# Four transformer layers on one core: VectorE's order in the full layers written out by urgency, and the weight check queued later

## The chip, the cores and the metric

The kernel runs on one core of one Trainium2 chip. The metric is the device time of one execution in microseconds (us); lower is better. Five engines work side by side, each takes its own instructions in their order: TensorE (PE, with its weight loads as PEld), VectorE (DVE), ScalarE (ACT), GpSimd (POOL) and SyncE (SP), which issues nearly all DMA transfers here. An instruction waits on semaphores until what it reads is there and what it overwrites is free.

## The reference

Four attention layers follow each other on x of shape [2048, 512]. Layers 0 and 2 use the weights A and see a window of 256 keys, layers 1 and 3 use the weights B and see all 2048 keys. There are 32 heads of 16.

```python
x = x + A(layernorm(x));  x = x + B(layernorm(x))
x = x + A(layernorm(x));  x = x + B(layernorm(x))

def A(x):  # B is the same without the mask
    q, k, v = (x @ wqkv) split into 32 heads of 16
    scores = q @ k.T / 4
    scores = where(0 <= i - j < 256, scores, -1e9)
    return (softmax(scores) @ v, heads joined) @ wo
```

## The kernel before, in words

**Numbers.** Weights and normalized inputs are split into a high and a low float16 part, and a product is the sum of three of the four part products (TERMS, L369). The kernel also checks its assumptions on the data: the smallest and largest softmax sum and the largest weights by column. All of it ends in one flag, and if the flag is not set, a slower general path computes the result.

**The full layers (1 and 3).** The loops run over four chunks of 512 queries (c) and eight groups of four heads (qd); in layer 3 the head groups are taken two at a time. For each of 16 key tiles there are two exps: 8 score matmuls into a PSUM tile of two banks (`exps`, L655 to L673, matmul line L664), one ScalarE exp over 128x1024 (L672), and 16 matmuls of values times exps that accumulate in two PSUM banks, `acc` (L716). After 16 key tiles `epilogue` (L624) adds the two halves of acc (`sa`, a join: two VectorE operations, L373 and L374), transposes them (L635), divides by the softmax sum (L638 to L645), transposes back (L648) and splits the result into float16 parts (L650, L651).

**Side work.** What the next layer needs is put between the exps: the output projection `wo` (L589) with residual add (L600) and the statistics of the next norm (L384, L385), `norm` (L387: scales by a Newton iteration, L45 to L51, then for each of four tiles two normalized copies and a difference, L398 and L404), the DMA transposes of the result (L425), and the projections of queries and keys (`project`, L433) and of values (`values`). In a full layer all side products share one PSUM tile, `halves` (L338, handed out by `bank`, L340). A product's first matmul may only start when the last product has been read out by the join on VectorE. `project` then splits j into two float16 parts (L465, L466), squares them (POOL, L471) and writes them to DRAM; `squares` (L484) and its readers get maxima of key and query norms, and the key maxima (km, L509) are taken from it.

**The weight check.** `verify` (L303) takes the eight matrices in turn. For each it loads four column blocks of 256 KB, one after another, into one buffer (`wc`, DMA at L309, `bufs=1`), and reduces each with one VectorE operation (L311); then it transposes the result (L314), reduces it again (L316) and updates the running minimum and maximum (L317, L318). That is 32 loads and 32 reduces. The check's works (CW) stand in the list of layer 1's side works, `side1`, and the first one depends on ("Q", 1, 2), the queries of chunk 2, which are made at the start of layer 1. The check's result is read only by the flag at the end.

**What sets the order.** The program is recorded by a planner with an estimated clock (`clock[0]`). In a full layer, each two exps move it to at least 1.8 us after the last two (L953). A side work is a generator that yields after each matmul or asks for a pause (`wait`); `Side.step` and `share` (L869 to L900) take from the list of works what is ready and what the budget for this step allows. PE executes in the order in which the planner recorded it (`manual_schedule`, L206). The other engines, VectorE among them, are ordered by the framework's own scheduler, which works from priorities (`high_priority(HEAD_START)` lifts urgent joins) and from its own estimate of the durations. So a VectorE instruction may be put ahead of ones that were recorded before it. All orders are fixed when the program is built.

`epilogue` is recorded through the queue `pvq`; `flush` empties it. `T` transposes a normalized chunk from the time XNR on, which `norm` sets to the planner's clock + 9 us.

Of the kernel before, what the change touches and what calls it, by code (L numbers as in the profile page):

```python
# [189 lines left out]
def fast_path(ctx, tc, flag, a_x, a_wqkv, a_wo, b_wqkv, b_wo, out):  # L190
# [29 lines left out]
    def wait(us):  # L220

        return "wait", clock[0] + us


# [78 lines left out]
    def verify(ty, s):  # L303

        am = vp.tile([P, D], F32, name=f"wa{ty}_{s}", tag="wa", bufs=1)
        for k in range(NC):
            f = slice(k * P, (k + 1) * P)
            raw = vp.tile([P, NC, P], F32, name=f"wc{ty}_{s}_{k}", tag="wc", bufs=1)
            nc.sync.dma_start(raw, mats[ty, s][:, f].rearrange("(k p) f -> p k f", p=P))  # L309
            yield wait(16)  # L310
            nc.vector.tensor_reduce(am[:, f], raw.rearrange("p k f -> p f k"), axis=AX.X, op=ALU.max, apply_absolute_value=True)  # L311
            yield wait(3)
        at = vp.tile([P, D], F32, name=f"wt{ty}_{s}", tag="wc", bufs=1)
        nc.vector.transpose(at, am)  # L314
        mx = vp.tile([P, D // 32], F32, name=f"wx{ty}_{s}", tag="wx")
        nc.vector.tensor_reduce(mx, at.rearrange("p (b r) -> p b r", r=32), axis=AX.X, op=ALU.max)  # L316
        nc.vector.tensor_tensor(wlow, wlow, mx, ALU.min)  # L317
        nc.vector.tensor_tensor(whigh, whigh, mx, ALU.max)  # L318
        yield wait(3)

# [50 lines left out]
    def join(dst, ps, scale=1 / WS):  # L371

        nc.vector.tensor_scalar(dst, ps[0], scale, None, op0=ALU.mult)  # L373
        nc.vector.scalar_tensor_tensor(dst, ps[1], scale, dst, op0=ALU.mult, op1=ALU.add)  # L374
# [12 lines left out]
    def norm(l, c, xs, tail=False):  # L387

        mv = ST[l, c][1]
        y = rsqrt(nc, vp, f"{l}_{c}", mv[:, :, 1])  # L390
        if tail:
            nb = vp.tile([P, 4], F32, name=f"nb{l}_{c}", tag="lnb", bufs=1)
            nc.vector.scalar_tensor_tensor(nb, mv[:, :, 0], -1.0, y, op0=ALU.mult, op1=ALU.mult)
        out = []
        for i in range(4):
            xn = vp.tile([P, D], F32, name=f"xn{l}_{c}_{i}", tag="xn", bufs=1)
            xh = vp.tile([P, 2, D], F16, name=f"xh{l}_{c}_{i}", tag="xh", bufs=XNB)
            norm1 = lambda o: nc.vector.tensor_scalar(o, xs[i], mv[:, i, 0:1], y[:, i:i + 1], op0=ALU.subtract, op1=ALU.mult)  # L398
            norm1(xn)
            if tail:  # L400
                nc.scalar.activation(xh[:, 0], xs[i], AF.Identity, bias=nb[:, i:i + 1], scale=y[:, i:i + 1])
            else:
                norm1(xh[:, 0])
            nc.vector.tensor_tensor(xh[:, 1], xn, xh[:, 0], ALU.subtract)  # L404
# [5 lines left out]
        return out  # L410

# [21 lines left out]
    def project(l, s, c, act, ht=None):  # L433
# [13 lines left out]
        for t in range(NHT) if ht is None else (ht,):  # L447
            ps = bank()
            w0 = t * P if ht is None else 0
            yield from mms(ps, [(w[:, k, a, w0:w0 + P], xc[:, b, k, :]) for a, b in TERMS for k in range(NC)], 2.2)  # L450
            if not PH["full"]:
                settle(not sqs)
            sp = vp.tile([P, 2, QC], F16, name=f"sp{n}_{t}", tag="sp", bufs=3)
            with tc.high_priority(HEAD_START):
                if PH["full"]:
                    j = vp.tile([P, QC], F32, name=f"j{n}_{t}", tag="j")
                    join(j, (ps[:, 0], ps[:, 1]))
                else:
                    if act:
# [4 lines left out]
            if PH["full"]:  # L464
                nc.vector.tensor_copy(sp[:, 0], j)  # L465
                nc.vector.tensor_tensor(sp[:, 1], j, sp[:, 0], ALU.subtract)  # L466
            sq = vp.tile([P, QC], BF16, name=f"sq{n}_{t}", tag="sq", bufs=NHT)
            if act:
                nc.scalar.activation(sq, sp[:, 0], AF.Square)
            else:  # L470
                nc.gpsimd.tensor_tensor(sq, sp[:, 0], sp[:, 0], ALU.mult)  # L471
            sqs[t] = sq

            d = dst[8 * t:8 * t + 8].rearrange("h (d b) n -> (h d) b n", b=4)
            if s:
                nc.sync.dma_start(d[:, 0:2], sp[:, 0:1].broadcast_to([P, 2, QC]))
                nc.sync.dma_start(d[:, 2], sp[:, 1])
            else:
                nc.sync.dma_start(d[:, 0:2], sp)
                nc.sync.dma_start(d[:, 2], sp[:, 0])  # L480
            yield -MM if PH["full"] else -12 * MM
        return sqs

    def squares(n, sqs):  # L484

        ph = bank()
        for t, sq in sqs.items():
# [101 lines left out]
    def wo(l, c, tail):  # L589
# [4 lines left out]
        for i in range(4):  # L594
# [6 lines left out]
            nc.sync.dma_start(xd[k], xs[i])  # L601
            stats(l + 1, c, i, xs[i])
            if i == 3:
                XN[l + 1, c] = norm(l + 1, c, xs, tail)
            yield -MM if PH["full"] else -12 * MM

    def wo_part(c, t):
# [6 lines left out]
        for i in range(4):  # L614
            ps = bank()
            yield from mms(ps, [(o[:, a, i * P:(i + 1) * P], w[:, b, :]) for a, b in TERMS])
            k = 4 * c + i
            with tc.high_priority(HEAD_START):
                for p in ((ps[:, 0], ps[:, 1]) if PH["full"] else (ps,)):
                    nc.vector.scalar_tensor_tensor(xs[i], p, 1 / WS, xs[i], op0=ALU.mult, op1=ALU.add)  # L620
            nc.sync.dma_start(out[0, k * P:(k + 1) * P, :] if t == NHT - 1 else xd[k], xs[i])
            yield -MM

    def epilogue(l, c, qd, a):  # L624
# [3 lines left out]
        n = f"{l}_{c}_{qd}"  # L628
        t, u = divmod(qd, 2)
        ot = vp.tile([P, QC // 32, 32], F32, name=f"ot{n}", tag="oe")  # L630
        with tc.high_priority(HEAD_START if l % 2 else 0):
            if l % 2:
                a = vp.tile([P, QC], F32, name=f"sa{n}", tag="j")
                join(a, acc, 1.0)
            nc.vector.transpose(ot.rearrange("p b r -> p (b r)"), a)  # L635
        den = ot[:, :, DH]

        nc.vector.tensor_tensor(lmin, lmin, den, ALU.min)  # L638
        nc.vector.tensor_add(lsum, lsum, den)
        r = vp.tile([P, QC // 32], F32, name=f"r{n}", tag="r")  # L640
        nc.vector.tensor_scalar_max(r, den, L_MIN)
        nc.vector.reciprocal(r, r)
        if u == 0:
            OT[t] = vp.tile([P, QC // 32, 2, DH], F32, name=f"op{n}", tag="op", bufs=1)
        nc.vector.tensor_tensor(OT[t][:, :, u, :], ot[:, :, :DH], r[:, :, None].broadcast_to([P, QC // 32, DH]), ALU.mult)  # L645
        if u:
            o = vp.tile([P, QC], F32, name=f"o{n}", tag="o", bufs=1)
# [4 lines left out]
            ONR[l, c, t] = clock[0] + 4.5  # L652


# [165 lines left out]
    class Side:  # L820
# [13 lines left out]
        def one(self, force=False):  # L834

            if PH["full"] and PH["busy"]:
                return self.piece(PH["last"])
# [84 lines left out]
    def attention(l, works):  # L922
# [5 lines left out]
        for t in range(NHT if l == 3 else 1):  # L928
            for c in range(NQ):
# [10 lines left out]
                for qd in qds:  # L940
# [5 lines left out]
                    began, u = clock[0], 0  # L946
                    for f in (attn_win if win else attn_full)(l, c, qd, *ops, a):
                        if f is None:
                            flush(1)
# [12 lines left out]
                        elif u:  # L962
                            sd.step()
                        u += 1
                    pvq[-1].append(lambda l=l, c=c, qd=qd, a=a: epilogue(l, c, qd, a))
# [3 lines left out]
                if not win:  # L969
                    settle()  # L970
        flush(0)
        phase(None)

# [32 lines left out]
    def NN(c, after=()):  # L1006
        def gen():
            xs = load_x(0, c)
            yield wait(12 if c > 1 else 0)
            for i in range(4):  # L1010
                stats(0, c, i, xs[i])
            XN[0, c] = norm(0, c, xs)
            yield 0.0
# [84 lines left out]
    def side1():  # L1098
# [25 lines left out]
    for l in range(4):  # L1124
# [48 lines left out]
```

## Time and profile before

| what | us |
|---|---|
| median of 3 runs (lowest, highest) | 2802.25 (2801.66, 2810.53) |
| the profiled execution | 2807.25 |
| span of its trace | 2805.5 |
| layer 1, from first to last exp | 516.25 to 1494.47 |
| layer 3 and its end | 1828 to 2793, end at 2805.5 |
| busy time of PE, ACT, DVE, POOL | 2507.0, 2364.1, 1085.8, 511.2 |
| mean granted clock of TensorE | 0.981 |

How to read it: a row of a timeline names the start, the duration, the engine, the line, the operation, the tile it writes and the tile it reads, partitions x elements; the number in square brackets is how long the engine stood idle before it, with what released it. x12 stands for twelve instructions merged into a row. "SPq" is the issue of a transfer by SyncE, and "DMA" is a transfer as a releaser.

### The profile page before, as it was taken

The numbers are of one execution on the slowest core, as the hardware profiler recorded it, in microseconds if no ns is written. First come the engines' busy times: TensorE is split into PE (matmuls) and PEld (weight loads), VectorE is DVE, ScalarE is ACT, GpSimd is POOL, SyncE is SP. The second block draws the span as 40 slices with busy tenths as digits, with TensorE's granted clock in tenths as the row PEclk, the third lists the DMA queues.
The fourth block names the chain that finished last, engine by engine and source line by source line (L and its number), as shares of the span: only waits on it lengthen the run. The fifth ranks groups of instructions, "written<-read, shape, count | busy, mean of one in ns | idle before, by whom it ended". The sixth has DMA issues, their size and how long they took to land.

```text
span 2805.5 us, 112293 instructions
## 1 busy us (share of the span) xinstructions
PE 2507.0 (89%) x50513; PEld 1101.9 (39%) x50513; DVE 1085.8 (39%) x2314; ACT 2364.1 (84%) x2683; POOL 511.2 (18%) x1074
## 2 busy tenths in 40 slices
PE   7889978698999999999899889889999999999897
PEld 3233434243444444444343333444444444433332
DVE  5564566322233223223335475613233233333233
ACT  4555644499999999999997667499999999999997
POOL 1445542000000000000013577300000000000000
PEclk9999989899999999999999999999999999999999
DMA  8887866422224223322324564633233233333333
GB/s 283 227 231 246 237 194 194 149 74 68 86 87 110 67 84 105 93 76 90 96 86 125 164 184 143 180 95 103 82 108 101 80 99 116 104 105 122 110 122 103
DMA packets 335035, 359.67 MB, mean 128 GB/s; under 512 B 113616, under 2 KB 250320, under 8 KB 328144
## 3 DMA queue, kind: packets, MB, share of 16 engines
q1 hardware_dynamic: 334544, 352.40, 41.4%
q8 instruction: 397, 6.50, 0.9%
q14 instruction: 94, 0.77, 0.1%
HBM read 239.60 MB, written 96.99 MB: 120 GB/s over the span
## 4 chain that ended last, share of the span: by engine, by line
ACT 52%; PE 21%; issue 11%; DVE 7%; DMA 6%; POOL 2%; SPq 0%; ACTq 0%; DVEq 0%; POOLq 0%
ACT e L672 51%; PE b L361 8%; PE acc L716 3%; PE acc L749 3%; PE s L664 2%; PE bs L361 2%; PE b L358 2%; PE s L668 1%; POOL e L739 1%; DMA wc<-in_A_wqkv_dram 1%; POOL e L742 1%; DMA wc<-in_B_wqkv_dram 1%; DVE wa L311 1%; DMA kt<-kw 1%; DVE ot L635 1%
## 5 line engine op out<-in xcount | busy, mean ns | idle before, releaser
L672 ACT ACTIVATE e<-s 128x1024 f32<-128x1024 f32 (+2 forms) x2432 | 2240.2, 1057 | 148.4 <-PE s L668 101.8
L716 PE MATMUL acc<-e,vt 64*17 64x512 f32 x16384 | 1091.0, 592 | 3.6 <-DVE sa L373 3.6
L664 PE MATMUL s<-qt,kt 64*32 64x512 f16 x16384 | 852.2, 381 | 131.2 <-ACT e L672 107.6
L664 PEld LDWEIGHTS <-kt 64*32 64x32 f16 x16384 | 406.4, 89 | 944.4 <-issue 869.8
L716 PEld LDWEIGHTS acc<-e,vt 64*17 64x17 f32 x16384 | 281.4, 92 | 68.4 <-DVE sa L373 3.9
L742 POOL TENSOR_SCALAR_AFFINE_SELECT e<-e 128x256 f32<-128x256 f32 x512 | 222.3, 441 | 197.9 <-ACT e L672 197.0
L739 POOL TENSOR_SCALAR_AFFINE_SELECT e<-e 128x256 f32<-128x256 f32 x448 | 196.5, 445 | 127.2 <-ACT e L672 125.8
L749 PE MATMUL acc<-e,vt 128*17 128x384 f32 (+2 forms) x2816 | 205.9, 399 | 10.8 <-DVE ot L635 6.3
L651 POOL TENSOR_TENSOR oh<-o,oh 128x512 f16<-128x512 f32 x31 | 36.1, 1163 | 964.6 <-DVE oh L650 927.7
L668 PE MATMUL s<-qt,kt 64*128 64x384 f16 (+2 forms) x1408 | 129.3, 280 | 63.4 <-ACT e L672 38.2
L361 PE MATMUL b<-xc,w 128*128 128x512 f16 x696 | 165.9, 390 | 8.2 <-DMA w<-wd 7.1
L373 DVE TENSOR_SCALAR sa<-acc 128x512 f32<-128x512 f32 x64 | 44.3, 692 | 318.7 <-PE acc L716 318.7
L620 DVE SCALAR_TENSOR_TENSOR x<-b,x 128x512 f32<-128x512 f32 x122 | 83.8, 687 | 196.9 <-PE b L358 189.7
L460 ACT ACTIVATE sp<-b 128x512 f16<-128x512 f32 x58 | 34.7, 598 | 112.8 <-PE b L361 97.9
L361 PEld LDWEIGHTS <-w 128*128 128x128 f16 x816 | 77.4, 100 | 128.9 <-issue 36.4
L668 PEld LDWEIGHTS <-kt 64*128 64x128 f16 x1408 | 54.5, 95 | 167.0 <-issue 136.6
L358 PE MATMUL b<-wo,oh 64*32 64x512 f16 x2592 | 110.5, 376 | 7.2 <-DVE x L620 4.9
L358 PE MATMUL b<-wv,xc 64*32 64x256 f16 (+1 forms) x3456 | 97.5, 309 | 20.8 <-DVE vt L374 19.3
L471 POOL TENSOR_TENSOR sq_h<-sp_h 128x512 bf16<-128x512 f16 x27 | 40.0, 1482 | 415.1 <-DVE sp_h L465 415.1
L471 POOL TENSOR_TENSOR sq<-sp 128x512 bf16<-128x512 f16 x28 | 40.0, 1428 | 406.1 <-DVE sp L465 365.4
L358 PE MATMUL b<-xc,w 64*32 64x512 f16 x2688 | 110.7, 376 | 2.8 <-DVE j L374 1.6
L358 PE MATMUL b<-xc,w_h 64*32 64x512 f16 x2592 | 103.3, 376 | 3.9 <-DVE km L509 3.9
(136 smaller groups left out, 1796.3 us busy)
## 6 DMA issues: line engine op xcount, KB each, us to landing
kt<-kf SPq DMA_DIRECT2D x128, 512.0 KB
qt<-qs SPq DMA_DIRECT2D x128, 256.0 KB
xd<-x SPq DMA_DIRECT2D x96, 256.0 KB
x<-xd SPq DMA_DIRECT2D x96, 256.0 KB
w<-wd SPq DMA_DIRECT2D x22, 1024.0 KB
kt<-kw SPq DMA_DIRECT2D x64, 256.0 KB
qs<-sp SPq DMA_DIRECT2D x48, 256.0 KB
wo<-wd SPq DMA_DIRECT2D x12, 1024.0 KB
```

Source lines behind the costliest of these rows:

```text
L358: nc.tensor.matmul(ps[g:g + 32, r], a[k, g:g + 32], b[k], start=(i == 0), stop=(i == len(pairs) - 1), skip_group_check=True)
L361: nc.tensor.matmul(ps, a, b, start=(i == 0), stop=(i == len(pairs) - 1))
L373: nc.vector.tensor_scalar(dst, ps[0], scale, None, op0=ALU.mult)
L471: nc.gpsimd.tensor_tensor(sq, sp[:, 0], sp[:, 0], ALU.mult)
L620: nc.vector.scalar_tensor_tensor(xs[i], p, 1 / WS, xs[i], op0=ALU.mult, op1=ALU.add)
L664: nc.tensor.matmul(ps[g:g + 32, h], kt[R * h:R * h + R, pr, kc + g:kc + g + 32], qt[R * h:R * h + R, pr], start=True, stop=True, skip_grou ...
L668: nc.tensor.matmul(ps[:, h, s0:s0 + wd_], kt[R * h:R * h + R, pr, kc:kc + P], qt[R * h:R * h + R, pr, qc:qc + wd_], start=True, stop=True)
L672: nc.scalar.activation(e[:, :, w0:w1], ps[:, :, w0:w1], AF.Exp, scale=SCALE)
L716: nc.tensor.matmul(acc[r][32 * h:32 * h + DH + 1, :], V[l, qd // 4, j // 8][k, j % 8, 4 * (qd % 4) + h, :], es_[h // 2][k, h % 2, :], star ...
L739: nc.gpsimd.affine_select(v, v, pattern=[[0, 2], [-1, P]], compare_op=ALU.is_gt, fill=0.0, base=0, channel_multiplier=1)
L742: nc.gpsimd.affine_select(v, v, pattern=[[0, 2], [1, P]], compare_op=ALU.is_ge, fill=0.0, base=0, channel_multiplier=-1)
L749: nc.tensor.matmul(a[32 * h:32 * h + DH + 1, q * P:(q + nb) * P], V[l, (4 * c + j) // 4][:, j % 4, 4 * qd + h, :], es_[h // 2][:, h % 2, s ...
```

## The change

1. **VectorE's order in the full layers.** Around `attention` of a full layer, VectorE is also taken in the order of recording, as PE is.

```python
-            attention(l, works[l] + [works[2][0] if l == 1 else [O3(3, 3)]])
+            with tc.manual_schedule(engines={mybir.EngineType.PE, mybir.EngineType.DVE}):
+                attention(l, works[l] + [works[2][0] if l == 1 else [O3(3, 3)]])
```

2. **Four queues and an estimated VectorE clock.** In a full layer, what is not urgent is not recorded at once but put into one of four queues. `vt_` estimates when VectorE is through with what has been recorded. `drain()` takes the next part of the first queue that isn't empty as long as that clock isn't over 0.2 us ahead of the planner's clock; `drain(n)` empties the first n queues at once.

```python
+    VQ, vt_ = [deque() for _ in range(4)], [0.0]
+    def vec(us):
+        vt_[0] = max(vt_[0], clock[0]) + us
+    def soon(chain, us, f):
+        if PH["full"]:
+            VQ[chain].append((clock[0], us, f))
+        else:
+            f()
+    def drain(upto=None):
+        if upto is not None:
+            for q in VQ[:upto]:
+                while q:
+                    vec(q[0][1])
+                    q.popleft()[2]()
+            return
+        while vt_[0] <= clock[0] + 0.2:
+            q = next((q for q in VQ if q), None)
+            if q is None:
+                return
+            vec(q[0][1])
+            q.popleft()[2]()
+    def turns(chain, *ops):
+        left = [len(ops)]
+        def one(f):
+            f()
+            left[0] -= 1
+        for us, f in ops:
+            soon(chain, us, lambda f=f: one(f))
+        while left[0]:
+            yield wait(0.5)
```

Recorded at once are the joins (`join` adds 1.4 us to vt_), the residual adds and the transpose of acc. Queue 0 holds the splits of queries and keys with their square and DMAs (1.2 us each); queue 1 the division and the split in `epilogue` (`scaled` 1.3, `parts` 1.2); queue 2 the statistics (0.9), the norm's scales (2.4) and its four tiles (1.8 each); queue 3 the check's reduces (1.1) and its end for a matrix (1.8). `drain()` is called before every step of side work, after every exp pair and each PE step; `drain(1)` before the join in `project` and in `squares`, `drain(2)` at the start of `epilogue`, and `drain(4)` at the end of a layer.

3. **The weight check.** Its reduces go through queue 3, and its wait after a load is 15 instead of 16 us of the planner's clock:

```python
-            yield wait(16)
-            nc.vector.tensor_reduce(am[:, f], ...)
-            yield wait(3)
+            yield wait(15)
+            yield from turns(3, (1.1, lambda: nc.vector.tensor_reduce(am[:, f], ...)))
...
+        yield from turns(3, (1.8, bounds))
```

4. **The norm** yields between its parts (`yield from turns(2, (2.4, scales), ...)`), and in a full layer the transposes may follow 2 instead of 9 us after it:

```python
-        XNR[l, c] = clock[0] + (0 if (l, c) == (0, 1) else 9)
+        XNR[l, c] = clock[0] + (0 if (l, c) == (0, 1) else 2 if PH["full"] else 9)
```

5. **The list of layer 1's side works.** The queries of layer 2 come a chunk later, ahead of the next keys:

```python
-            a += [OO(1, c), T(2, c), K(2, c, False), VV(2, c, False)] + ([Q(2, c, False)] if c < 2 else [])
+            a += [OO(1, c), T(2, c)] + ([Q(2, c - 1, False)] if c else []) + [K(2, c, False), VV(2, c, False)]
```

The arithmetic and the number of instructions on the tensors are the same.

More of the change, by code (lines that the diff above doesn't have):

```diff
@@ L408, in norm @@
                 out.append(xh)
-        XNR[l, c] = clock[0] + (0 if (l, c) == (0, 1) else 9)
-        return out
+        yield from turns(2, (2.4, scales), *[(1.8, lambda i=i: parts(i)) for i in range(4)])
+        XN[l, c] = out
+        XNR[l, c] = clock[0] + (0 if (l, c) == (0, 1) else 2 if PH["full"] else 9)
     def load_x(l, c):
@@ L458, in project @@
                 else:
+                    sp = vp.tile([P, 2, QC], F16, name=f"sp{n}_{t}", tag="sp", bufs=3)
                     if act:
@@ L484, in squares @@
     def squares(n, sqs):
+        drain(1)
+        vec(1.4)
         ph = bank()
@@ L601, in wo @@
             nc.sync.dma_start(xd[k], xs[i])
-            stats(l + 1, c, i, xs[i])
-            if i == 3:
-                XN[l + 1, c] = norm(l + 1, c, xs, tail)
+            vec(1.4)
+            soon(2, 0.9, lambda i=i: stats(l + 1, c, i, xs[i]))
+            if i == 3 and not PH["full"]:
+                yield from norm(l + 1, c, xs, tail)
             yield -MM if PH["full"] else -12 * MM
+        if PH["full"]:
+            yield from norm(l + 1, c, xs, tail)
     def wo_part(c, t):
@@ L629, in epilogue @@
         t, u = divmod(qd, 2)
+        drain(2)
         ot = vp.tile([P, QC // 32, 32], F32, name=f"ot{n}", tag="oe")
@@ L652, in epilogue @@
             ONR[l, c, t] = clock[0] + 4.5
+        soon(1, 1.3, scaled)
+        if u:
+            soon(1, 1.2, parts)
     def exps(name, kt, qt, pr, pieces):
@@ L834, in one @@
         def one(self, force=False):
+            drain()
             if PH["full"] and PH["busy"]:
@@ L963, in attention @@
                             sd.step()
+                        drain()
                         u += 1
@@ L971, in attention @@
         flush(0)
+        drain(4)
         phase(None)
@@ L1011, in gen @@
                 stats(0, c, i, xs[i])
-            XN[0, c] = norm(0, c, xs)
+            yield from norm(0, c, xs)
             yield 0.0
```

98 lines of the change are left out of this document (54 added, 44 removed).

## The prediction

> **What bounds the kernel now.** I read the page first, then the stretches of the four layers, then the waits of VectorE, then the timeline at each place where an engine that should not stop stops. From the page come two lines, the engines' shares and the chain of work that ended last:
>
> ```profile
> PE 2507.0 (89%) x50513; PEld 1101.9 (39%) x50513; DVE 1085.8 (39%) x2314; ACT 2364.1 (84%) x2683; POOL 511.2 (18%) x1074
> ACT 52%; PE 21%; issue 11%; DVE 7%; DMA 6%; POOL 2%; SPq 0%; ACTq 0%; DVEq 0%; POOLq 0%
> ```
>
> VectorE (DVE) works 39% of the time and still holds 7% of the chain. An engine that is mostly idle does that only by being late at single places, and those places are what this change can touch. The next view gives the stretches: start, length, then busy time and instructions of PE, PEld, DVE, ACT and POOL, the granted clock and the DMA share.
>
> ```profile
> core 0: us, PE busy (x) PEld busy (x) DVE busy (x) ACT busy (x) POOL busy (x), PEclk, DMA share, GB/s
> 350.00:516.00 166.00, 139.64 (x1100) 64.80 (x1097) 98.31 (x200) 72.87 (x106) 46.99 (x120) 0.95 0.67 203
> 516.00:556.00 40.00, 20.73 (x540) 9.60 (x528) 12.55 (x19) 22.79 (x26) 0.00 (x0) 0.82 0.33 99
> 556.00:1494.00 938.00, 872.13 (x21968) 392.65 (x21975) 272.02 (x577) 921.34 (x1000) 58.42 (x46) 0.99 0.27 84
> 1828.00:2793.00 965.00, 874.07 (x21629) 384.88 (x21626) 310.37 (x594) 945.17 (x1025) 57.46 (x42) 1.00 0.33 103
> ```
>
> The full layers (rows 2 and 3 are layer 1, row 4 is layer 3) are paced by ScalarE's exps: 921.34 of 938 us busy. So a full layer can win only what ACT stands idle: 938 - 921.34 = 16.7 us in the long row and 40 - 22.79 = 17.2 us in the short one, 33.9 us in all of layer 1. Row 1 is the tail of layer 0, where PE (139.64 of 166) sets the pace and 26 us are idle. The next rows are the check's groups of instructions and two waits of PE on VectorE (us in total, times, longest).
>
> ```profile
> L311 DVE TENSOR_REDUCE wa<-wc 128x128 f32<-128x512 f32 x32 | 33.5, 1047 | 65.6 <-DMA wc<-in_B_wqkv_dram 31.1 <-DMA wc<-in_A_wqkv_dram 16.9 <-DMA wc<-in_B_wo_dram 10.9
> L314 DVE STREAM_TRANSPOSE wt<-wa 128x512 f32<-128x512 f32 x8 | 5.7, 707 | 0.1
> L316 DVE TENSOR_REDUCE wx<-wt 128x16 f32<-128x512 f32 x8 | 5.4, 681 | 0.2
> PE b L358 <- DVE vt L374: 20.4, 3, 14.1
> PE b L361 <- DVE x L600: 3.4, 3, 1.2
> ```
>
> The 32 reduces of the weight check work 33.5 us but hold VectorE a further 65.6 us, because VectorE takes its instructions in order and stands at each of them until its 256 KB load has landed. Whatever is queued behind waits too.
>
> **The change part by part.** What it moves, by the two instruction orders: ScalarE's order stays the same, so do the PE orders of layers 0, 2 and 3. Of the check, the first load stays, its 31 others move on SP's queue from the tail of layer 0 and the first steps of layer 1 into layer 1, and all 32 reduces on DVE stand between exp 220 and exp 844 of layer 1's 1024. In layer 1 side work on PE moves too (queries of one chunk ahead of the keys of the next).
>
> *a) The tail of layer 0.* DVE rows of the norm, and PE and SP rows that follow from it:
>
> ```profile
> 386.36 0.17 DVE L46 TENSOR_SCALAR y<-v 128x4 int32<-128x4 int32 x1
> 391.13 1.08 DVE L311 TENSOR_REDUCE wa<-wc 128x128 f32<-128x512 f32 x1 [4.60 <-DMA wc<-in_A_wqkv_dram]
> 401.15 1.91 PE L749 MATMUL acc<-e,vt 128*17 128x128 f32 x16 [5.52 <-DVE ot L635]
> 404.33 0.76 SPq L327 DMA_DIRECT2D w<-wd  x1
> 410.14 8.02 PE L361 MATMUL b<-xc,w 128*128 128x512 f16 x24 [7.09 <-DMA w<-wd]
> 473.63 1.47 PE L361 MATMUL b<-wv,xc 128*128 128x256 f16 x12 [1.08 <-DVE x L600]
> 478.89 1.47 PE L361 MATMUL bs<-xc,w 128*128 128x512 f16 x6 [3.79 <-DMA w<-wd]
> ```
>
> A normalization is cut in two by a reduce: DVE is at L46 at 386.53, then idle 4.60, then 1.08 in the reduce. Behind it stand the rest of the norm, the transpose out of PSUM (L635) for which PE idles 5.52, and, on SP, the transposes of the normalized tile, behind which SP issues the weight load (404.33) for which PE idles 7.09. These two PE gaps are one delay seen twice: when DVE is 4.60 + 1.08 = 5.7 us earlier, the first gap goes, PE comes to the second earlier, and the second shrinks only as far as the load is earlier. So I count 5.7, not 12.6. Ahead of that the three waits for x L600 are 3.4 us (joins that stood behind reduces); they go. At 478.89 PE waits 3.79 us for a load that SP issues after the DVE work of the same place; I take it as gone. Sum 5.7 + 3.4 + 3.8 = 12.9, **-13 us**. Bounds: 5.7 alone, -6, if the small waits are replaced by the next releaser; if both long gaps vanish, 5.52 + 7.09 + 3.4 + 3.79 = -20.
>
> [...] The profile's chain shows the clock after that gap:
>
> ```profile
> 410.14 5.31 PE b L361 x12
> 507.90 2.59 PE b L361 x12
> ```
>
> Twelve equal matmuls took 5.31 us right after 7.09 idle us, 2.59 us elsewhere. I count none of these 2.7 us as won, since a long wait for the load remains in my case. [...]
>
> *b) The start of layer 1.* DVE, then PE, then ACT:
>
> ```profile
> 521.08 1.10 DVE L311 TENSOR_REDUCE wa<-wc 128x128 f32<-128x512 f32 x1 [14.48 <-DMA wc<-in_B_wqkv_dram]
> 531.25 1.02 DVE L311 TENSOR_REDUCE wa<-wc 128x128 f32<-128x512 f32 x1 [2.85 <-DMA wc<-in_B_wqkv_dram]
> 532.19 0.41 DVE L373 TENSOR_SCALAR vt<-b 128x256 f32<-128x256 f32 x1
> 533.11 1.05 PE L358 MATMUL b<-wv,xc 64*32 64x256 f16 x32 [5.13 <-DVE vt L374]
> 558.96 0.84 PE L358 MATMUL b<-wv,xc 64*32 64x256 f16 x24 [14.15 <-DVE vt L374]
> 534.72 1.02 ACT L672 ACTIVATE e<-s 128x1024 f32<-128x1024 f32 x1 [5.52 <-PE s L664]
> 536.85 1.02 ACT L672 ACTIVATE e<-s 128x1024 f32<-128x1024 f32 x1 [1.11 <-PE s L664]
> 560.35 1.02 ACT L672 ACTIVATE e<-s 128x1024 f32<-128x1024 f32 x1 [14.33 <-PE s L664]
> 562.48 1.94 ACT L672 ACTIVATE e<-s 128x1024 f32<-128x1024 f32 x2 [1.11 <-PE s L664]
> ```
>
> The joins of the values (vt, L373/L374) empty the one PSUM bank that side work has in a full layer. They stand behind reduces that wait for loads; PE's next side matmul waits for the join, the score matmuls stand behind it, and ACT has no scores: 5.52 + 1.11 + 14.33 + 1.11 = 22.1 us. With no check instruction before exp 220 these joins find DVE empty. I take 21 of the 22.1, leaving a microsecond for the first join.
>
> *c) Inside layer 1.* DVE, PE and ACT around the epilogue of one tile:
>
> ```profile
> 1375.37 0.69 DVE L404 TENSOR_TENSOR xh<-xn,xh 128x512 f16<-128x512 f32 x1
> 1375.97 0.69 DVE L373 TENSOR_SCALAR sa<-acc 128x512 f32<-128x512 f32 x1
> 1376.71 2.13 PE L716 MATMUL acc<-e,vt 64*17 64x512 f32 x9 [3.62 <-DVE sa L373]
> 1380.23 4.02 ACT L672 ACTIVATE e<-s 128x1024 f32<-128x1024 f32 x4 [5.76 <-PE s L664]
> ```
>
> The join of acc stands behind a whole norm. In the changed order the norm's parts are in queue 2 and the join precedes them: 5.76 goes, less at most one part already begun (0.69 by the row), so 5.2. The remaining idle time of ACT in the long stretch is 16.7 less the last gap's share after 556 (560.35 - 556 = 4.35), less 1.11 and 5.76, that is 5.5 us in pieces under 1 us; of these I take 1.5. Together b) and c): 21 + 5.2 + 1.5 = 27.7, **-28 us**. Bounds: -20 (b alone, a little less), -33.9 (all of ACT's idle time).
>
> *d) What is added there.* The check itself: 33.5 + 5.7 + 5.4 = 44.6 us of DVE, and two small operations for each matrix, of which some 12 lay in layer 1 already (the 12.55 us of the 516 row are nearly all check); DVE there goes from 285 to about 320 of 978 us. Reduces that find their data cost nothing on the path. Two rows bound how late a load can be:
>
> ```profile
> 384.61 6.50 DMA wc<-in_A_wqkv_dram
> 421.81 2.71 DMA wc<-in_A_wqkv_dram
> ```
>
> A check load took 2.7 to 6.5 us from issue to use, and this in a tail with a DMA share of 0.67; layer 1 has 0.27. In the changed order each reduce but one stands at least 12 exps behind its load, that is 12 x 921.34/1000 = 11 us, over 4 us more than the slowest of the two; the exception stands 32 exps ahead of the next urgent join. So I take 0; if that cover is gone, each one blocks DVE for about 3.9 us (2.85 + 1.02, rows above). SP's queue: the loads stand between loads of keys and queries whose own lead does not change. Queue 1 parts that `drain` puts ahead of a join in layer 1 cost the join at most some 2.5 us, and the join's lead in the order is 3 to 4 exps, 2.8 to 3.7 us: 0, with 1 to 3 us lost if it is short (inside the bounds).
>
> *e) The boundary to layer 2.* PE and ACT:
>
> ```profile
> 1493.06 2.36 PE L358 MATMUL b<-wv,xc 64*32 64x512 f16 x80
> 1497.50 1.51 ACT L672 ACTIVATE e<-s 128x768 f32<-128x768 f32 x2 [3.03 <-PE s L668]
> ```
>
> 80 side matmuls are left after the last exp, 2.36 us. In the changed order the last side matmul stands 4 steps ahead of it: **-2.4**; bounds 0 and -3.03.
>
> *f) Layer 3, layer 2, the rest of layer 0.* Layer 3 has no check, and only a few adds change places; its 965 - 945.17 = 19.8 us of ACT's idle time hang on key maxima and their chain over POOL, which stays as it is: 0, bounds -1 and +2. Layer 2 and the front of layer 0: 0.
>
> Sum: -13 - 28 - 2.4 = -43.4, taken as -44 with the half microsecond of layer 3. The profiled execution took 2807.25 us, 1.75 more than its span of 2805.5; against it the forecast is 2763. The median of the runs is 2802.25, 5.0 lower; the order of each engine is the same in every run, so I carry the whole sum over: **2758 us**.
>
> **The rivals.** *Rival A, the tail of layer 0 gives little back.* The 7.09 gap shows that the weight load is what PE meets last, and a load issued from SP depends on more than DVE: if SP's place or the free buffer decides, only 3 of the 13 us come. For it: a weight load ends two of the gaps, and in the changed order that of 404.33 stands behind all four transposes of the tile, before behind three. Against: those transposes wait for the very norm that is held up. Time: 2758 + 10 = 2768, and 2776 if half of e) and the small pieces of c) fail too.
>
> *Rival B, the check's wait comes back in layer 1.* The DVE order there is fixed by an estimated clock; where the real engines run ahead of it, a reduce stands in front of a join again. For it: b) shows 22 us lost in just this way. Against: 11 us of lead. With half of b) and c) lost again: 2758 + 14 to 28, 2772 to 2786; if the tail fails as well, 2796.
>
> *Rival C, slower.* In layer 1 the single PSUM bank makes each late join a stop of ACT. If check loads are issued late by SP (its queue is in order, and a load of keys that waits for a free buffer stands ahead of them), each reduce holds DVE for 2.85 + 1.02 = 3.9 us in front of a join, and the fixed order cannot step aside, where before part of the check lay in the tail, off ACT's path. It decides from 44 / 3.9 = 11 to 12 of the 32 reduces on; with 20 of them 2758 + 78 = 2836. Against it: the lead of 11 us again, and a DMA share of 0.27.
>
> *Rival D, it does nothing.* If the profile's waits on check loads were only where DVE had nothing else to do, removing them would change nothing: 2802. Against: the ACT gaps of 5.52 and 14.33 us stand in the rows of the engine that sets the pace.
>
> **How the numbers follow.** The forecast (2746 to 2770) 0.62; A beyond it (to 2776) 0.12; B 0.15, of it 0.02 over 2793; C 0.07; D 0.04. The predicted time is the forecast's, 2758. Lower end: -20 - 33.9 - 3 = -57, 2745. Upper end: A and the half-lost B, 2784. About 0.3% (8.4 us) is what a measurement of this kernel can tell from no change. Faster than 2794: forecast, A and most of B, 0.87; within the bound D and 0.02 of B, 0.06; slower C, 0.07.
>
> **What would show it.** a) PE's wait before the first matmuls of the tail's query weights shorter and 5 to 8 us earlier on the clock; layer 1's first exp at about 503 instead of 516. b) No wait of PE for vt over 1.5 us, and ACT without gaps over 2 us from there to exp 220. c) No wait of PE for sa of 3 us. d) Waits of L311 on its loads near 0 in layer 1, and the stretch from first to last exp of layer 1 some 950 us instead of 978. e) No run of side matmuls behind the last exp. f) Layer 3 within 2 us of 965. The prediction is wrong if L311 still waits for loads beside gaps of ACT, if the tail's gap for w is as late as before, or if joins in layer 1 wait behind drained parts.

## The result and the profile after

The changed kernel takes 2758.35 us (median of 4 runs, 2757.74 to 2759.5), the kernel before 2803.81 us (4 runs, 2801.66 to 2810.53): ratio 0.9834 with a 95% interval of 0.9817 to 0.9852. The forecast was 2758. The profiled executions differ by 2805.5 - 2757.7 = 47.8 us of span, and the trace says in which stage. The table takes the starts of four exps (the 157th, the first of layer 1, of layer 2 and of layer 3) from each trace:

| stage, us | before | after | difference |
|---|---|---|---|
| start to the 157th exp | 368.12 | 364.87 | -3.3 |
| 157th exp to the first of layer 1 (tail of layer 0) | 148.14 | 130.64 | -17.5 |
| first exp of layer 1 to the first of layer 2 | 981.24 | 952.98 | -28.3 |
| first exp of layer 2 to the first of layer 3 | 331.70 | 335.11 | +3.4 |
| first exp of layer 3 to the end | 976.32 | 974.10 | -2.2 |

This table turns out to be the better instrument: in the fourteen profiles of this study the first row lies anywhere between 364.9 and 370.9 us, whichever kernel runs, while the tail lies between 130.1 and 131.3 us in all twelve that have no check in it, and layer 1 of the one program that was profiled twice (a_free, a_best) differs by 0.6 us. So the first row, and with it a good part of what whole times differ by below some 5 us, says nothing on the change.

From the page of the changed kernel the engines' shares and the chain:

```profile
PE 2496.1 (91%) x50513; PEld 1100.3 (40%) x50513; DVE 1094.9 (40%) x2314; ACT 2362.9 (86%) x2683; POOL 515.8 (19%) x1074
ACT 56%; PE 23%; issue 11%; DVE 5%; DMA 3%; POOL 2%; SPq 0%; ACTq 0%; DVEq 0%; POOLq 0%
```

VectorE does the same work (1094.9 us, 1085.8 before) and holds 5% of the chain instead of 7%, DMA 3% instead of 6%. The stretches (columns as in the prediction):

```profile
350.00:495.50 145.50, 135.01 (x1071) 63.07 (x1070) 68.54 (x154) 70.61 (x103) 47.89 (x117) 0.98 0.64 191
495.50:535.00 39.50, 35.80 (x1103) 18.46 (x1104) 6.47 (x16) 39.50 (x45) 0.00 (x0) 1.00 0.22 70
535.00:1448.00 913.00, 853.11 (x21488) 382.41 (x21464) 313.77 (x624) 904.34 (x982) 59.46 (x46) 1.00 0.31 95
1783.00:2745.00 962.00, 872.27 (x21622) 386.25 (x21622) 312.32 (x592) 943.97 (x1024) 57.52 (x42) 1.00 0.33 103
```

The second row is the clearest: in its first 39.5 us layer 1 keeps ACT busy all 39.5 (22.79 of 40 before), with 6.47 us of VectorE. The column of the granted clock moves too: 0.95, 0.82 and 0.99 in the first three rows before, 0.98, 1.00 and 1.00 now. Then the check's own groups and its only wait, and PE's waits on what used to stop it:

```profile
L350 DVE TENSOR_REDUCE wa<-wc 128x128 f32<-128x512 f32 x32 | 34.6, 1082 | 2.6 <-DMA wc<-in_A_wqkv_dram 2.6
DVE wa L350 <- DMA wc<-in_A_wqkv_dram: 2.6, 1, 2.6
PE b L402 <- DMA w<-wd: 5.8, 1, 5.8
PE b L399 <- DVE vt L416: 0.8, 1, 0.8
```

65.6 us of waiting at loads have become 2.6, and PE's 20.4 us for vt 0.8. The wait for the weight load in the tail is still there, 5.80 us instead of 7.09, as the prediction had it, but it ends at 397.24 instead of 410.14 us from the start (3.3 of these 12.9 us are the first row of the table).

The epilogue that stopped ACT for 5.76 us, in the changed kernel: VectorE, then ACT.

```profile
1330.68 0.69 DVE L415 TENSOR_SCALAR sa<-acc 128x512 f32<-128x512 f32 x1 [5.13 <-PE acc L779]
1331.48 0.69 DVE L416 SCALAR_TENSOR_TENSOR sa<-acc,sa 128x512 f32<-128x512 f32 x1
1321.61 15.84 ACT L735 ACTIVATE e<-s 128x1024 f32<-128x1024 f32 x17
```

The join waits only for PE, no norm is in front of it, and 17 exps follow each other without a gap. What is lost against that stands in the same layer, at each of seven places; VectorE, PE and ACT of one of them:

```profile
1212.18 0.69 DVE L415 TENSOR_SCALAR sa<-acc 128x512 f32<-128x512 f32 x1 [11.13 <-PE acc L779]
1213.70 0.71 DVE L694 STREAM_TRANSPOSE ot<-sa 128x512 f32<-128x512 f32 x1
1214.34 0.65 DVE L415 TENSOR_SCALAR vt<-b 128x512 f32<-128x512 f32 x1
1215.77 0.62 PE L399 MATMUL b<-xc,w 64*32 64x512 f16 x16 [0.76 <-DVE vt L416]
1216.74 2.10 ACT L735 ACTIVATE e<-s 128x1024 f32<-128x1024 f32 x2 [0.54 <-PE s L727]
```

A side product's join stands behind the join and transpose of acc, comes about 2 us late, and ACT loses 0.54 us. Seven of them are 3.8 us; with a pause of PE of 1.31 us for which the trace shows no reason, and smaller ones, the changed kernel loses 6.4 us against the kernel before, exp by exp, between the 26th and the 775th exp of layer 1. The run a_xnr9 below shows which part of the change brings most of this loss.

At the end of layer 1 the side matmuls behind the last exp are gone (PE, then ACT):

```profile
1445.61 2.52 PE L779 MATMUL acc<-e,vt 64*17 64x512 f32 x32
1448.49 2.76 PE L402 MATMUL b<-xc,w 128*128 128x512 f16 x12
1448.50 1.51 ACT L735 ACTIVATE e<-s 128x768 f32<-128x768 f32 x2 [1.47 <-PE s L731]
```

### The profile page after: what moved, and what is told of

The parts are those of the page before. It is cut to its first block, busy times and chain, and to the rows that moved or that the text cites. A ratio compares the mean times of both kernels' runs of the same rounds, so it can differ in the third digit from the quotient of the medians.

```text
span 2757.7 us, 112292 instructions
## 1 busy us (share of the span) xinstructions
PE 2496.1 (91%) x50513; PEld 1100.3 (40%) x50513; DVE 1094.9 (40%) x2314; ACT 2362.9 (86%) x2683; POOL 515.8 (19%) x1074
## 4 chain that ended last, share of the span: by engine, by line
ACT 56%; PE 23%; issue 11%; DVE 5%; DMA 3%; POOL 2%; SPq 0%; ACTq 0%; DVEq 0%; POOLq 0%
ACT e L735 55%; PE b L402 10%; PE acc L812 3%; PE acc L779 3%; PE bs L402 2%; PE s L731 2%; PE s L727 2%; PE b L399 1%; POOL e L802 1%; POOL e L805 1%; DMA qt<-qs 1%; DMA kt<-kw 0%; DMA wr<-in_A_wo_dram 0%; DVE ot L694 0%; DMA w<-wd 0%
## 5 line engine op out<-in xcount | busy, mean ns | idle before, releaser
L415 DVE TENSOR_SCALAR j_h<-b 128x512 f32<-128x512 f32 x27 | 18.7, 691 | 218.7 <-PE b L399 187.6
```

## The experiments

The theory after the result: VectorE standing in order at the check's loads cost the tail of layer 0 and the start of layer 1, and the change wins by moving the check. The rivals: the fixed order as such wins; the queues win; the shorter waits or the new list of side works win. All ratios are against the kernel before on the same chip. The table repeats the stages of each profile, in us:

| run | median | ratio (interval) | tail of layer 0 | layer 1 | layer 3 to end |
|---|---|---|---|---|---|
| changed kernel | 2758.35 | 0.9834 (0.9817-0.9852) | 130.6 | 953.0 | 974.1 |
| b_nocheck | 2763.31 | 0.9839 (0.9819-0.9860) | 130.3 | 957.6 | 976.6 |
| a_nocheck | 2758.51 | 0.9824 (0.9805-0.9843) | 130.7 | 955.0 | 974.2 |
| b_manual | 2801.36 | 0.9988 (0.9978-0.9997) | 130.1 | 978.1 | 989.9 |
| a_auto | 2799.85 | 0.9975 (0.9961-0.9989) | 146.0 | 975.9 | 975.4 |
| a_noq1 | 2802.91 | 0.9997 (0.9987-1.0006) | 130.6 | 981.6 | 990.0 |
| a_noq2 | 2767.58 | 0.9871 (0.9853-0.9889) | 130.9 | 959.8 | 974.4 |
| a_oldlist | 2765.56 | 0.9857 (0.9841-0.9873) | 131.3 | 959.2 | 974.2 |
| a_wait2 | 2756.55 | 0.9825 (0.9809-0.9842) | 131.2 | 952.3 | 975.0 |
| a_batch | 2806.20 | 0.9999 (0.9987-1.0010) | 131.0 | 999.4 | 974.2 |
| a_xnr9 | 2755.54 | 0.9827 (0.9810-0.9843) | 131.0 | 947.8 | 974.5 |
| a_free | 2753.29 | 0.9811 (0.9795-0.9828) | 130.2 | 949.4 | 974.9 |
| a_best | 2760.81 | 0.9838 (0.9825-0.9851) | 130.6 | 948.8 | 975.8 |

**The check left out, in both kernels** (b_nocheck, a_nocheck):

```
-        a = [CW(*x, [("C", *y)] if y else [("Q", 1, 2)]) for y, x in zip([None] + m, m)]
+        a = []
```

> The kernel before without the weight check (leaves out its 32 loads, 32 reduces and 8 closings; the bounds keep their start values). Theory (VectorE standing in order at the check's loads costs the tail of layer 0 and the start of layer 1): both come back, by the two traces 17.5 us from exp 156 to the first exp of layer 1 and 23.4 us in the next 26 exps, so 2803 - 41 = 2762 us, 2756 to 2768; the stall of 5.76 us before acc (1374 us in the trace before) stays. Rival (the order of VectorE in layer 1 is what wins, the check's waits hide other delays): over 2785.

> The changed kernel without the weight check (leaves out the same). Theory (in layer 1 the check is fully covered): within 3 us of the changed kernel's 2758, so 2755 to 2761. Rival (the reduces, 48 us of VectorE, still delay joins in layer 1, where the changed kernel lost 6.4 us against the kernel before between exp 486 and 902): 2748 to 2753.

Measured: 2763.31 and 2758.51 us. Taking only the check out of the kernel before brings 42 us, nearly all of the change; the tail is 130.3 us, the same as with the change. And in the changed kernel the check costs nothing that can be measured. The theory stands on both; the late joins of 0.54 us are not the check's doing, since they are there without it. The stall behind the norm stays in b_nocheck (6.29 us), as expected, so it is not the check's; that it is gone in the changed kernel is won besides.

**One half of the change at a time** (b_manual, a_auto):

```
 b_manual, in the kernel before:
-            attention(l, works[l] + [...])
+            with tc.manual_schedule(engines={mybir.EngineType.PE, mybir.EngineType.DVE}):
+                attention(l, works[l] + [...])
 a_auto, in the changed kernel:
-            with tc.manual_schedule(engines={mybir.EngineType.PE, mybir.EngineType.DVE}):
+            if True:
```

> The kernel before with one edit: VectorE in the order of recording in the full layers; no queues, old list, old waits. In this order the check's reduces move behind the start of layer 1. Theory (the check's place is nearly all of it): 2803 - 41 = 2762, plus some us since whole norms stand ahead of joins, 2760 to 2775. Rival (the queues by urgency carry the gain): 2785 or more.

> The changed kernel with VectorE ordered by the framework again; queues, waits and list as changed. In the built order the check's reduces stand where the kernel before had them. Theory (only the fixed order moves the check): 2795 to 2806, as before. Rival (queues, shorter waits or the new list win by themselves): 2760 to 2785.

Measured: 2801.36 and 2799.85. Each half alone is worth 4 to 6 us. For the queues without the fixed order that was expected: the framework puts the reduces back into the tail (146.0 us) and the start of layer 1. For the fixed order without queues it was not, and my theory as I had put it falls here. The tail has its 18 us (130.1), and the start of layer 1 too: exp by exp the run is 43 us ahead of the kernel before when layer 1's 26th exp starts. Then it loses 20 us in the rest of layer 1 and 14 in layer 3, where there is no check at all. VectorE (first and last of a norm of 24 instructions, and the join), PE and ACT of the largest place:

```profile
1341.48 0.17 DVE L45 TENSOR_SCALAR v<-mv 128x4 f32<-128x4 f32 x1
1350.21 0.69 DVE L404 TENSOR_TENSOR xh<-xn,xh 128x512 f16<-128x512 f32 x1
1350.82 0.68 DVE L373 TENSOR_SCALAR sa<-acc 128x512 f32<-128x512 f32 x1
1351.56 2.73 PE L716 MATMUL acc<-e,vt 64*17 64x512 f32 x16 [6.62 <-DVE sa L373]
1354.82 2.85 ACT L672 ACTIVATE e<-s 128x1024 f32<-128x1024 f32 x3 [8.51 <-PE s L664]
```

In the order of the source a whole norm of 9.4 us stands in front of the join of acc. So nearly all of the gain has one source, the check's place, and two conditions: the fixed order brings it, the queues keep the fixed order from costing nearly as much again.

**Which queue** (a_noq1, a_noq2): the parts of one queue are recorded at once.

```
-        if PH["full"]:
+        if PH["full"] and chain != 1:      # a_noq2: chain != 2
             VQ[chain].append((clock[0], us, f))
```

> The changed kernel without queue 1: the division and the split of an epilogue are recorded at once. Theory (joins of side products then stand behind 4 us of epilogue instead of 2, in layers 1 and 3): 10 to 25 us lost, 2768 to 2783. Rival (a side product leaves 2 us of room and that is enough): 2755 to 2763.

> The changed kernel without queue 2: statistics and norms of a full layer are recorded at once and whole, ahead of what follows. Theory (the queues are what makes the fixed order cost nothing; the kernel before with the fixed order alone stopped ACT for 8.5 us at 1346 us behind a whole norm): 5 to 12 us lost, 2763 to 2770. Rival (norms are rare, three in layer 1, and meet no join): 2755 to 2761.

Measured: 2802.91 and 2767.58. Queue 2, for the norms, is worth what was expected, 9 us, of it 6.8 in layer 1. Queue 1, for the epilogue's division and split, is worth 45 us, nearly twice the expected upper end: 28.6 in layer 1 and 15.9 in layer 3. One place in a_noq1 (VectorE, PE, ACT):

```profile
1050.27 0.71 DVE L694 STREAM_TRANSPOSE ot<-sa 128x512 f32<-128x512 f32 x1
1052.99 0.43 DVE L711 CAST oh<-o 128x512 f16<-128x512 f32 x1
1053.33 1.41 DVE L653 SCALAR_TENSOR_TENSOR x<-b,x 128x512 f32<-128x512 f32 x2
1054.80 1.06 PE L399 MATMUL b<-wo,oh 64*32 64x512 f16 x16 [3.21 <-DVE x L653]
1056.41 1.02 ACT L735 ACTIVATE e<-s 128x1024 f32<-128x1024 f32 x1 [3.64 <-PE s L727]
1058.54 1.02 ACT L735 ACTIVATE e<-s 128x1024 f32<-128x1024 f32 x1 [1.11 <-PE s L727]
```

Between the transpose and the residual add stand 2.4 us of small operations (from 1050.98 to 1053.33). They delay the side product's read-out by that, and it costs 3.64 + 1.11 = 4.75 us of ACT: the matmuls after the gap run slower (1.06 us for 16, 0.62 at the place shown of the changed kernel; the trace's granted clock is 0.50 from 1053.9 to 1060.7 us), so that ACT stops a second time. My estimate lacked these second stops, but they are only part of the miss: stretches with a clock of 0.50 and a second stop of about 1 us stand at five places of layer 1 and at one of layer 3. At the other places ACT stops once, mostly for 1 to 1.9 us.

**The price of a late reduce** (a_wait2, a_batch): once as it comes, with a wait of 2 us behind each load, once with all four loads and reduces of a matrix straight in front of a join of a side product.

```
 a_wait2:
-            yield wait(15)
+            yield wait(2)
 a_batch (verify records one batch for a matrix and puts it in queue 3;
 drain() looks at queues 0 to 2 only):
     def join(dst, ps, scale=1 / WS):
+        if ps is not acc and VQ[3]:
+            VQ[3].popleft()[2]()
```

> The changed kernel with the check's wait after a load cut from 15 to 2 us of the planner's clock, so that each reduce stands right behind its load in VectorE's order. The price of rival C by itself. Theory (a fixed order needs the lead of 11 us): VectorE waits 1 to 4 us at most of the 32 reduces, a third of them hold a join, 2768 to 2800. Rival (VectorE is idle enough, so a late reduce holds nobody): 2756 to 2763.

> The changed kernel with the check in eight batches, each recorded straight ahead of a join of a side product in layer 1: four loads into the one buffer and their reduces, so that three of the four wait for a transfer with the join behind them. The price of rival C with the place it speaks of. Theory (what costs is a wait between a side product and its join, not a wait of VectorE as such): each batch holds VectorE for some 3 x 3.9 + 1 + 1.7 = 14 us, of which 9 to 11 reach ACT, 72 to 90 us in all, 2825 to 2850. Rival (layer 1 has room for VectorE's waits wherever they stand, as the run with the short wait after a load suggests): 2756 to 2775.

Measured: 2756.55 and 2806.20. In both VectorE stands long at the loads (us in total, times, longest; first a_wait2, then a_batch):

```profile
DVE wa L350 <- DMA wc<-in_A_wqkv_dram: 20.8, 6, 5.8
DVE wa L350 <- DMA wc<-in_B_wqkv_dram: 19.3, 8, 3.0
DVE wa L350 <- DMA wc<-in_B_wo_dram: 8.4, 2, 6.1
DVE wa L350 <- DMA wc<-in_A_wo_dram: 7.6, 3, 2.6
```

```profile
DVE wa L352 <- DMA wc<-in_A_wqkv_dram: 30.1, 9, 4.4
DVE wa L352 <- DMA wc<-in_B_wqkv_dram: 27.0, 9, 4.0
DVE wa L352 <- DMA wc<-in_B_wo_dram: 11.1, 3, 4.6
DVE wa L352 <- DMA wc<-in_A_wo_dram: 9.3, 3, 3.7
PE b L401 <- DVE j L420: 32.1, 7, 8.4
```

56 us of waiting cost nothing in a_wait2 (its layer 1 is 952.3 us, the changed kernel's 953.0); 78 us in a_batch cost 46 us of layer 1. The difference is the last row: only in a_batch does PE wait for a join behind them, five times for 2.46 to 8.41 us (the row's other two waits are of 0.76 us, as the changed kernel has them; a sixth, 2.65 us, is shown in the last section). So the theory of the short wait failed, and the lead of 11 us that the prediction leaned on is not what protects the changed kernel. It is the place: in a_wait2 PE's waits for joins in layer 1 are the eight of 0.76 us that the changed kernel has too (seven of them are the late joins above). That queue 3 is what keeps this place free, since it is given out last, is argued: no run records its parts at once. a_batch shows the price of a bad place, together with that of four loads in a row, at 46 us instead of the 72 to 90 expected: behind six of the eight batches PE waits 33.3 us in all, so the room between a product and the next one took up more of the 14 us than I had allowed.

**The list and the transposes** (a_oldlist, a_xnr9): each as before.

```
 a_oldlist:
-            a += [OO(1, c), T(2, c)] + ([Q(2, c - 1, False)] if c else []) + [K(2, c, False), VV(2, c, False)]
+            a += [OO(1, c), T(2, c), K(2, c, False), VV(2, c, False)] + ([Q(2, c, False)] if c < 2 else [])
 a_xnr9:
-        XNR[l, c] = clock[0] + (0 if (l, c) == (0, 1) else 2 if PH["full"] else 9)
+        XNR[l, c] = clock[0] + (0 if (l, c) == (0, 1) else 9)
```

> The changed kernel with the list of layer 1's side works as before (queries of a chunk right after its values). Theory (the list is worth nothing by itself): within 4 us of 2758, and the wait of PE for the second chunk's query load in layer 2, 3.76 us in the changed kernel's trace, is again 2.7 us. Rival (the list is what keeps side matmuls from being left after the last exp): 2761 to 2766 with a run of some 80 side matmuls at the end of layer 1.

> The changed kernel with 9 instead of 2 us between a norm and its transposes in a full layer, as before. Theory (no transfer of layer 1 is on the path): within 4 us of 2758. Rival (the earlier transposes are what let the side work of layer 1 end before the last exp): 2761 to 2768 with side matmuls after the last exp.

Measured: 2765.56 and 2755.54. With the old list two runs of side matmuls stand behind the last exp, and ACT waits 8.11 us where the changed kernel waits 1.47:

```profile
1449.45 2.78 PE L399 MATMUL b<-wv,xc 64*32 64x512 f16 x96
1453.77 2.78 PE L399 MATMUL b<-wv,xc 64*32 64x512 f16 x96 [1.54 <-DVE vt L416]
```

The rival is right there: the new list is worth 6.2 us of layer 1. PE's wait for the second chunk's queries is 3.08 us with the old list and not 2.7 as expected. The transposes' earlier time wins nothing; layer 1 is even 5.2 us shorter with the old one (947.8). That tells where the 6.4 us in the middle of layer 1 come from: from its 26th to its 775th exp a_xnr9 takes 692.5 us, the kernel before 692.0, the changed kernel 698.4. Of the seven late joins two stand at the same exps and one elsewhere, and the stop of ACT behind PE's pause of 1.31 us is gone. a_nocheck takes 698.7 us there and a_auto, which has the shorter wait without the fixed order, 697.9. So most of this loss goes with the shorter wait, not with the check or with VectorE's fixed order; by which steps of the planner was not followed.

**A version that might beat both** (a_free, and a_best, which is the same program measured again): a join tells the planner when VectorE will be through with it.

```
     def join(dst, ps, scale=1 / WS):
         vec(1.4)
+        if dst is not None and ps is not acc:
+            PH["free"] = max(PH["free"], vt_[0] + 0.9)
```

> The changed kernel with one addition: a join sets the earliest time of the next side product to the estimated VectorE clock + 0.9 us instead of the planner's clock + 2.0 us alone. Theory (the nine stops of ACT of 0.54 us and the like in layer 1 are side products whose join stands behind the join and transpose of acc): these go and 3 to 6 us are won, 2752 to 2755. Rival (the side work is only put off and stands at the end of the layer): 2757 to 2762.

> The changed kernel with the addition of a_free once more, in five rounds, to settle its few us. Theory (the stops of ACT behind late joins are real and gone): 3 to 6 us under the changed kernel, 2752 to 2755. Rival (within what runs differ): 2756 to 2760.

Measured: 2753.29 and 2760.81. Layer 1 is 3.6 and 4.1 us shorter than in the changed kernel, both times, and of the seven stops of 0.54 us behind late joins three are left in each of the two traces. But the whole time does not settle it: the ratios 0.9811 and 0.9838 lie on both sides of the changed kernel's 0.9834, the first stage of the second profile being 4.5 us longer than that of the first (370.9 and 366.4). What is shown is the gain in the stage; that the kernel is faster as a whole stays open. The two edits that shorten layer 1, this one and the old time of the transposes, were not run together; both win in the same stretch (693.0 us in a_free and 692.4 in a_best from the 26th to the 775th exp, 692.5 in a_xnr9), so their gains need not add up.

## Why the prediction was right, point by point

**a) The tail of layer 0**: forecast -13, measured -17.5, inside the bounds of -6 to -20; b_nocheck shows that the check is all of it (130.3 us without it). By the exps, the small waits up to the norm gave 2.4 (2.3 of the forecast), the norm and the load behind it 8.2 (5.7), the rest up to layer 1 6.9 (4.9). The mechanism was right and the term of the norm too small: I counted only the wait and the reduce that cut it (5.7 us). The norm also had a second reduce in it (1.03 us at 402.23), and in the kernel before its last tile is done at 404.44, in the changed kernel at 389.02: 15.4 us earlier, of which 5.6 had been won ahead of it. VectorE in the kernel before (end of the norm):

```profile
403.79 0.65 DVE L404 TENSOR_TENSOR xh<-xn,xh 128x512 f16<-128x512 f32 x1
```

VectorE in the changed kernel (start of the norm, its end), and PE after the load:

```profile
376.87 0.26 DVE L45 TENSOR_SCALAR v<-mv 128x4 f32<-128x4 f32 x1
388.30 0.72 DVE L448 TENSOR_TENSOR xh<-xn,xh 128x512 f16<-128x512 f32 x1
397.24 7.11 PE L402 MATMUL b<-xc,w 128*128 128x512 f16 x24 [5.80 <-DMA w<-wd]
```

The weight load comes 12.9 us earlier. 24 matmuls take 7.11 us there after 5.80 us idle (8.02 before, after 7.09), against 12 in 2.76 us at the start of layer 2, so most of the slow stretch after the gap is still paid; I had counted nothing of it as won, and 0.9 us was.

**b) and c) Layer 1 up to its last exp, and e) the boundary**: forecast -28 and -2.4, measured -28.3 for both together. The start gave 23.4 (21 forecast), the epilogue behind the norm 6.0 (5.2), the boundary 1.6 (2.4). Small pieces gave 3.5 (1.5), but 6.4 were lost in the middle of the layer, 3.8 of them at joins behind the join and transpose of acc. Step d) had allowed 1 to 3 us for another delay, parts of queue 1 ahead of a join; at none of the seven places does one stand there. The prediction put the shorter wait before the transposes, with which most of the loss goes, at nothing without a word. Errors of both signs, so the sum was better than its terms.

**d) The check is covered in layer 1**: right, as a_nocheck shows. The reason given, 11 us of lead, does keep the waits away (2.6 us in all), but it is not what makes the check free: a_wait2 has no such lead, waits 56 us and loses nothing. So the 3.9 us for each late reduce, at which rival C reckoned, are no price by themselves.

**f) Layers 2 and 3**: forecast 0, measured +3.4 and -2.2. The 3.4 lie at the load of the second chunk's queries and the matmuls behind it (before, then after):

```profile
1548.86 0.82 PE L668 MATMUL s<-qt,kt 64*128 64x384 f16 x4 [2.66 <-DMA qt<-qs]
1550.60 6.13 PE L361 MATMUL b<-xc,w 128*128 128x512 f16 x24
```

```profile
1500.96 0.82 PE L731 MATMUL s<-qt,kt 64*128 64x384 f16 x4 [3.76 <-DMA qt<-qs]
1502.70 7.34 PE L402 MATMUL b<-xc,w 128*128 128x512 f16 x24
```

1.1 us of longer wait and 1.2 us of a longer slow stretch. The stage lies between 332.3 and 335.1 us in the profiles with a deferred check, so part of it is not the change's. The wait is 3.77 us in b_nocheck too, which has neither the new list nor the fixed order, so these do not make it; what does stays open.

**The total.** The sum was -44, the medians differ by 45.5. That the forecast came within half a microsecond of the measured time is partly luck: -17.5 stands for -13, -28.3 for -30.4, +1.2 for 0, and the first row's -3.3, which says nothing on the change, for 0. Two small slips stand in the sum itself: 5.76 - 0.69 is 5.1 and not 5.2, and the half microsecond that makes -44 of -43.4 is put down to layer 3, to which step f) gives 0.

**The rivals.** A (the tail gives little) and D (nothing happens) are refuted by the stages. B's joins came late by little, 3.8 us, through the join and transpose of acc and not through the check. C does not happen here, but a_batch shows its mechanism: 46 us. What the prediction missed as a rival is the fixed order itself: without the queues it gives nearly all of the gain back (2801.36 us, 4 below the kernel before). I had read the queues as something that costs up to 2.5 us, and not as what pays for the order; the total came out because the queues are there.

## What to carry to other kernels

In these runs an instruction that waited for a transfer cost by what stood behind it in its engine's order and not by how long it waited: the same check cost 42 us in front of joins and norms, and nothing, with 56 us of waiting, where nothing was due. Whoever takes an order into their own hands has to bring the urgency too, since source order puts long runs of work that can wait in front of the one short instruction that releases the pacemaker; here that was worth nearly as much as the whole gain. And when a few microseconds matter, compare the stages of the traces, since the whole time also carries stages that vary by themselves (here the first, 364.9 to 370.9 us).

## What the runs showed of the hardware

At one place of these runs a stop of PE cost more than its length (4.75 us of ACT for 3.21 us, a_noq1), and of two stops of nearly equal length one had slow matmuls behind it and one had not. After 3.21 us of idle time in a_noq1, 16 matmuls took 1.06 us instead of 0.62; after 2.66 us in layer 2 of the kernel before, matmuls were slow too (24 in 6.13 us, against 12 in 2.76). In a_batch, after 2.65 us, they were not; its rows after a gap of 7.18 us stand below for comparison:

```profile
705.08 0.41 PE L547 MATMUL b<-sq,hsum 64*32 64x512 bf16 x8 [2.65 <-DVE j L420]
705.31 0.40 PE L731 MATMUL s<-qt,kt 64*32 64x512 f16 x8
```

```profile
899.64 1.05 PE L401 MATMUL b<-xc,w 64*32 64x512 f16 x16 [7.18 <-DVE j L420]
900.45 0.67 PE L731 MATMUL s<-qt,kt 64*32 64x512 f16 x8
```

8 score matmuls took 0.40 us after the one gap and 0.67 after the other. The granted clock tells the two nearly equal stops apart. Two stretches of 3.40 us around each of them (the kernel before, then a_batch; columns as in the prediction: PE's busy time stands behind the length of 3.40 us, the clock is third from the end):

```profile
1545.40:1548.80 3.40, 0.80 (x8) 0.09 (x4) 1.76 (x6) 1.64 (x2) 3.02 (x8) 1.00 1.02 372
1548.80:1552.20 3.40, 3.34 (x16) 0.89 (x17) 0.00 (x0) 1.51 (x2) 1.48 (x4) 0.50 0.93 317
```

```profile
700.80:704.20 3.40, 1.48 (x32) 0.50 (x31) 3.24 (x6) 2.85 (x4) 0.00 (x0) 1.00 0.00 0
704.20:707.60 3.40, 2.38 (x64) 0.92 (x65) 3.21 (x6) 1.71 (x2) 1.48 (x1) 1.00 0.53 167
```

The stop of 2.66 us lies almost whole in the first of its two stretches, PE is busy for 0.80 of the 3.40 us, and the clock of the second is 0.50. The stop of 2.65 us is split between its two stretches, PE is busy for 1.48 us in the first, and the clock is 1.00 in both. What decides when the clock goes down was not shown. In the changed kernel's place shown above a stop of PE of 0.76 us cost ACT 0.54 us, and the matmuls behind it were not slow (16 in 0.62 us).
